# Agent attention and a squared-gate layer on one core: scores and agent values as two 64-column halves, and eight key groups ahead of tile 0

## The chip, the core and the metric

The program runs on one core of one Trainium2 chip. The core has a matrix engine (TensorE; PE in the profile, its weight loads PEld), VectorE (DVE), ScalarE (ACT), GpSimd (POOL), and SyncE (SP), which issues every DMA of this kernel. The metric is the device time of one execution in microseconds (us), lower is better. The kernel before ran three times: 1067.81, 1068.59 and 1078.64 us, median 1068.59.

## What is computed

```python
B, N, C, n_agents = 2, 12480, 128, 49
def sm(a, b):                       # row softmax of scaled scores
    s = (a @ b.transpose(0, 2, 1)) / np.sqrt(C)
    e = np.exp(s - s.max(-1, keepdims=True))
    return e / (e.sum(-1, keepdims=True) + 1e-09)
agent_v = sm(agents, k) @ v         # per batch: 49 x 128
attn = sm(q, agents) @ agent_v      # per batch: 12480 x 128
x = attn.reshape(B * N, C)          # 24960 tokens
h = x @ w_in                        # 128 -> 2048
g = np.where(h >= 1, h, np.where(h <= -1, 0, (h + 1) ** 2 / 4))
out = g @ w_out                     # 2048 -> 128
```

The weights w_in and w_out are 64-bit floats that the kernel decodes itself. All else is float32. A plain float32 matmul is two matmul instructions (each with its own weight load) on the engine; the large products of the second layer are instead split into a high and a low part of a rounded type (fp32r), one instruction each.

## The kernel before

The tokens of both batches are cut into 49 **tiles** of 512 (tile 24 holds the border between the batches, tile 48 has 384). The keys of one batch are 98 blocks of 128, in 14 **groups** of 7 (KG = 7), and the values likewise.

**Startup (batch 0).** For each key group: load (448 KB), scores of the 7 blocks against the agents on PE (L510; the block is the stationary operand, 128 columns; the agents of both batches, 98 columns, stream), copy to `ks` on ACT, running maximum on DVE. Then subtract the maximum (POOL), exponential (ACT), and agent values (L634: 98 columns of `ks` stationary, 129 columns of a value block streaming, summed in PSUM over the 7 blocks of a group and added to `acc` on DVE). From `acc` the agent values `av` are formed, transposed, multiplied with w_in (L699) and split into `w_hi` and `w_lo`. DVE, ACT and POOL decode w_in and w_out beside this.

**A tile.** Its query scores are four blocks (L958: a query block is stationary, 49 agent columns stream); maximum, subtraction, sum and reciprocal on DVE (L973 to L991), exponential on ACT, product on POOL (L996), four transposes on PE (L1009), copies on ACT and DVE to `mt`. Then eight pairs of hidden blocks: first product on PE (L1086; 49 of the 128 rows of the array for each of two row halves, which run side by side), relu and square on ACT (L1094, L1099), gate on DVE (L1102), high part on POOL or DVE, low part on POOL or DVE (L1113), second product on PE (L1126; two row halves of 64). ACT and DVE collect `total`, and SP stores it.

**Rides (batch 1).** The key and value groups of batch 1 are worked off between tiles 3 and 24: in each tile the query scores of the next tile (q) and the transposes of this one (tr) stand next to each other on PE, and each of the two places can carry one **ride**, a key group (L766, 7 matmuls), a value group (L859, 7 matmuls) or a step of what follows them. The order of the rides is the list `order` in `second_batch`; 14 key groups come first, then the maximum, then 14 value groups, then the product with w_in.

**What sets the order.** Every step is an `Op` with its engine, a cost in us, what it depends on and a key. `Order.run` lays them out once, engine by engine, by these numbers (START, NEXT and TIMES hold the keys), and each engine works its list in order. A PE step with another number of array rows than the one before costs `SWITCH` in the plan. On the chip nothing is reordered: an instruction that waits holds up all behind it on its engine.

## Time and profile before

| | value |
|---|---|
| median of three runs | 1068.59 us |
| the profiled execution, its own time | 1067.88 us |
| its span | 1066.0 us |
| PE busy | 1048.2 us (98%) |
| ACT busy | 900.6 us (84%) |
| DVE busy | 860.8 us (81%) |
| POOL busy | 700.6 us (66%) |

The span is the time from the first to the last instruction of the profile; 1.9 us of the profiled execution lie outside it. Busy times are unions over an engine's instructions. Matmuls are pipelined and the ends of their rows are modelled, so a stretch of matmuls is read by the distance from one start to the next. PEclk is the granted clock of TensorE as a share of full speed.

### The profile page before, as it was taken

To read this page: it belongs to the slowest core of one execution; us is meant where nothing else is said; L and a number is where in the kernel's file an instruction comes from. 1 tells how busy PE (TensorE), PEld (TensorE's weight loads), DVE (VectorE), ACT (ScalarE), POOL (GpSimd) and SP (SyncE) were. 2 spreads that over 40 slices of the span, in tenths; PEclk is the share of its full clock that TensorE was granted. 3 is DMA by queue.
4 is the path that set the end of the run, shared out by engine and by line. 5 is a ranking of instruction groups with operands and counts; after the bars stand their busy time and mean duration, and the time that the engine had idled before them with its cause. 6 is when DMAs were issued, how large, how long until landed. Compare 5 with 4: busy or idle time off the path is not lost.

```text
span 1066.0 us, 20344 instructions
## 1 busy us (share of the span) xinstructions
PE 1048.2 (98%) x8117; PEld 797.8 (75%) x8117; DVE 860.8 (81%) x1071; ACT 900.6 (84%) x1003; POOL 700.6 (66%) x442
## 2 busy tenths in 40 slices
PE   7989999999999999999999999999999999999997
PEld 6956777877777777777777877777777777777776
DVE  6677777777887777788888888888888888888886
ACT  2357888778988888799899899999999999999995
POOL 2745666556785676656667767677676776766765
PEclk9979999999999999999999999999999999999999
DMA  9931111200012111000010100101001000000000
GB/s 310 403 141 38 56 55 57 81 30 21 21 52 79 56 56 56 31 30 22 20 41 22 31 30 21 40 21 31 30 21 40 21 30 32 21 28 11 11 21 18
DMA packets 23710, 56.90 MB, mean 53 GB/s; under 512 B 2752, under 2 KB 3136, under 8 KB 23616
## 3 DMA queue, kind: packets, MB, share of 16 engines
q1 hardware_dynamic: 23616, 55.60, 15.4%
q8 instruction: 64, 1.05, 0.4%
q14 instruction: 30, 0.25, 0.1%
HBM read 42.81 MB, written 12.78 MB: 52 GB/s over the span
## 4 chain that ended last, share of the span: by engine, by line
PE 88%; ACT 3%; DVE 2%; POOL 2%; issue 2%; DMA 1%; POOLq 0%; SPq 0%; DVEq 0%; ACTq 0%
PE total L1126 50%; PE ph L1086 23%; PE ph L958 5%; PE ph L859 2%; PE ph L766 2%; PE ph L634 2%; PE ph L1009 2%; ACT g L1094 1%; POOL glo L1113 1%; ACT g L1099 1%; POOL ghi L322 1%; DVE g L1102 1%; PE ph L510 1%; DMA raw<-w_out 1%; DMA kbuf<-kT 0%
## 5 line engine op out<-in xcount | busy, mean ns | idle before, releaser
L1102 DVE SCALAR_TENSOR_TENSOR g<-g,ph 128x1024 f32<-128x1024 f32 (+1 forms) x392 | 470.0, 1210 | 109.3 <-ACT g L1099 87.1
L1094 ACT ACTIVATE g<-ph,half 128x1024 f32<-128x1024 f32 (+1 forms) x392 | 423.7, 1106 | 11.2 <-PE ph L1086 2.8
L322 POOL CAST ghi<-g 128x1024 fp32r<-128x1024 f32 (+1 forms) x196 | 250.5, 1278 | 242.3 <-DVE g L1102 234.3
L1099 ACT ACTIVATE g<-g 128x1024 f32<-128x1024 f32 (+1 forms) x392 | 402.2, 1053 | 6.2
L1113 POOL TENSOR_TENSOR glo<-g,ghi 128x1024 fp32r<-128x1024 f32 (+1 forms) x147 | 352.9, 2401 | 66.9 <-PE ph L958 43.6
L1086 PE MATMUL ph<-mt,w_hi 49*128 49x512 f32 (+2 forms) x1600 | 270.8, 416 | 4.9 <-DVE g L1102 3.8
L1126 PE MATMUL total<-ghi,wo_hi 64*128 64x512 f32 (+1 forms) x1176 | 205.4, 426 | 0.8 <-POOL ghi L322 0.8
L1086 PEld LDWEIGHTS ph<-mt,w_hi 49*128 49x128 f32 x1600 | 151.1, 187 | 64.1 <-issue 22.0
L1126 PE MATMUL total<-g,wo 64*128 64x512 f32 (+1 forms) x784 | 185.4, 591 | 0.1
L1126 PE MATMUL total<-ghi,wo_lo 64*128 64x512 f32 (+1 forms) x1176 | 185.0, 391 | 0.0
L1113 DVE TENSOR_TENSOR glo<-g,ghi 128x1024 fp32r<-128x1024 f32 (+1 forms) x147 | 177.1, 1231 | 1.9 <-POOL ghi L322 1.9
L1126 PE MATMUL total<-glo,wo_hi 64*128 64x512 f32 (+1 forms) x1176 | 174.0, 401 | 0.2 <-POOL glo L1113 0.2
L1086 PE MATMUL ph<-mt,w_lo 49*128 49x512 f32 (+2 forms) x800 | 157.8, 388 | 0.0
L1126 PEld LDWEIGHTS total<-ghi,wo_hi 64*128 64x128 f32 x1176 | 112.8, 185 | 44.1 <-issue 22.6
L1126 PEld LDWEIGHTS total<-ghi,wo_lo 64*128 64x128 f32 x1176 | 112.4, 184 | 24.0
L1126 PEld LDWEIGHTS total<-glo,wo_hi 64*128 64x128 f32 x1176 | 108.4, 186 | 27.3 <-POOL glo L1113 0.6
L1126 PEld LDWEIGHTS total<-g,wo 64*128 64x128 f32 x784 | 75.3, 187 | 55.3 <-issue 46.2
L1086 PEld LDWEIGHTS ph<-mt,w_lo 49*128 49x128 f32 x800 | 77.0, 186 | 15.9
L996 POOL TENSOR_TENSOR pq<-qd,qsm 128x392 f32<-128x392 f32 (+1 forms) x49 | 58.0, 1184 | 25.4 <-DVE qsm L991 25.4
L324 DVE CAST ghi<-g 128x1024 fp32r<-128x1024 f32 (+1 forms) x98 | 71.0, 725 | 1.8
L958 PEld LDWEIGHTS ph<-ag,qt 128*128 128x128 f32 (+1 forms) x392 | 48.0, 193 | 21.2 <-issue 20.7
L958 PE MATMUL ph<-ag,qt 128*128 128x49 f32 (+1 forms) x392 | 54.0, 282 | 4.4 <-DMA qt<-qT 4.4
(102 smaller groups left out, 611.7 us busy)
## 6 DMA issues: line engine op xcount, KB each, us to landing
qt<-qT SPq DMA_DIRECT2D x48, 256.0 KB, 2.7
outT<-ot SPq DMA_DIRECT2D x48, 256.0 KB, 2.0
kbuf<-kT SPq DMA_DIRECT2D x27, 448.0 KB, 4.8
vbuf<-v_in SPq DMA_DIRECT2D x18, 451.5 KB, 4.2
ghi<-v_in SPq DMA_DIRECT2D x5, 451.5 KB, 7.9
glo<-v_in SPq DMA_DIRECT2D x5, 451.5 KB, 9.1
raw<-w_in SPq DMA_DIRECT2D x4, 512.0 KB, 5.8
raw<-w_out SPq DMA_DIRECT2D x4, 512.0 KB, 7.9
```

The costliest lines, as they stand in the source:

```text
L322: pool.tensor_copy(out, in_)
L324: dve.tensor_copy(out, in_)
L634: nc.tensor.matmul(out=one(PS["v", b, g])[0:A2, 0:C + 1], lhsT=ksf[:, g, t * A:t * A + A2], rhs=vb[0][:, t, :], start=t == 0, stop=t == KG ...
L766: nc.tensor.matmul(out=ps[:, t * A:(t + 1) * A], lhsT=kb[:, t * SUB:(t + 1) * SUB], rhs=ag[:, b, :], start=True, stop=True,)
L958: nc.tensor.matmul(out=ps[lo:hi, i * A:(i + 1) * A], lhsT=st["q"][:, i * 128 + lo:i * 128 + hi], rhs=ag[:, b, :], start=True, stop=True,)
L996: (pool if e == "POOL" else dve).tensor_tensor(out=pq[:, :, :, 0:A], in0=d.unsqueeze(2).to_broadcast([128, ns, 2, A]), in1=st["sm"].unsque ...
L1086: nc.tensor.matmul(out=st["h"][:, c, lo:hi], lhsT=W[b][w][r, f:f + 128], rhs=M[j][r, x, lo:hi], start=(i == 0), stop=(i == 2),)
L1094: act.activation(out=st["g"], in_=st["h"][:, :, 0:n], func=ACTF.Relu, bias=half, scale=0.5)
L1099: act.activation(out=st["g"], in_=st["g"], func=ACTF.Square)
L1102: dve.scalar_tensor_tensor(out=st["g"], in0=st["g"], scalar=1.0, in1=st["h"][:, :, 0:n], op0=ALU.min, op1=ALU.max,)
L1113: (pool if e == "POOL" else dve).tensor_tensor(out=st["lo"], in0=st["g"], in1=st["hi"].bitcast(F32), op=ALU.subtract)
L1126: nc.tensor.matmul(out=total[:, i, 0:n], lhsT=w[r, f, :], rhs=x[r, c, :], start=begins, stop=LEFT[j] == 0,)
```

## The change

Three things are changed, and the plan is laid out anew with other keys.

1. Scores (of queries and of keys) and agent values use the array as two halves of 64 columns. A score block of 128 columns becomes two matmuls of 64 columns, which write PSUM rows 0 to 63 and 64 to 127 (`columns`). For the agent values, blocks alternate between the two halves, each half sums its own blocks, and DVE adds both halves to `acc`, in two additions where there was one (`beside`, `join_halves`). The stationary operand is 64 columns instead of 98.
2. Eight of the 14 key groups of batch 1 (`early`) run before and during the first products of tile 0, into the PSUM of `total`, with 98 streaming columns; the first second product waits for the last of them (`early_op`). Six groups remain as rides, and the rides behind them move up by eight places.
3. The loads have other keys: key loads now stand first in SP's queue, ahead of w_in, and the query tiles of the startup come later; eight early key loads stand in the startup where there were four.

```diff
+EARLY = 8
-    ag = const.tile([128, B, A], F32, name="ag")
+    ag = const.tile([128, B + 1, A], F32, name="ag")
+    def columns(ps, lhsT, rhs, lo=0, hi=128):
+        for c in range(lo, hi, 64):
+            nc.tensor.matmul(
+                out=ps[c:c + 64], lhsT=lhsT[:, c - lo:c - lo + 64], rhs=rhs, start=True, stop=True
+            )
+    def beside(ps, g, vt, lo, hi):
+        for t in range(lo, hi):
+            c = 64 * (t % 2)
+            nc.tensor.matmul(
+                out=ps[c:c + 64, 0:C + 1], lhsT=ksf[:, g, t * A:t * A + 64], rhs=vt[:, t, :],
+                start=t < 2, stop=t >= KG - 2,
+            )
+    def join_halves(o, ps, first):
+        if first:
+            dve.tensor_copy(acc, ps[0:A, 0:C + 1])
+        else:
+            dve.tensor_tensor(out=acc, in0=acc, in1=ps[0:A, 0:C + 1], op=ALU.add)
+        dve.tensor_tensor(out=acc, in0=acc, in1=ps[64:64 + A, 0:C + 1], op=ALU.add)
...
             def weigh(ps):
                 st["ps"] = ps
-                for t in range(KG):
-                    nc.tensor.matmul(
-                        out=ps[0:A2, 0:C + 1], lhsT=ksf[:, g, t * A:t * A + A2],
-                        rhs=vb[:, t, :], start=t == 0, stop=t == KG - 1,
-                    )
+                beside(ps, g, vb, 0, KG)
...
+        def early(g):
+            kb = kbuf[(b * NG + g) % BUFS["k"]]
+            ps = total[:, g % 2, :]
...
+            def scores(o, e, lo=0, hi=HALF):
+                for t in range(lo, hi):
+                    columns(
+                        ps[:, t * A:t * A + A2], kb[:, t * SUB:(t + 1) * SUB], agf[:, A:A + A2]
+                    )
...
-        for g in range(NG):
-            keys(g, g)
-        maximum(NG + 2)
-        for g in range(NG):
-            values(g, NG + 5 + g)
-        return form(2 * NG + 6)
+        for g in range(EARLY):
+            early(g)
+        for g in range(EARLY, NG):
+            keys(g, g - EARLY)
+        n = NG - EARLY
+        n += n % 2
+        maximum(n + 2)
+        for g in range(NG):
+            values(g, n + 5 + g)
+        return form(n + NG + 6), late["early"]
...
             for i, b, lo, hi in bl:
-                nc.tensor.matmul(
-                    out=ps[lo:hi, i * A:(i + 1) * A],
-                    lhsT=st["q"][:, i * 128 + lo:i * 128 + hi],
-                    rhs=ag[:, b, :],
-                    start=True,
-                    stop=True,
+                columns(
+                    ps[:, i * A:(i + 1) * A], st["q"][:, i * 128 + lo:i * 128 + hi], ag[:, b, :],
+                    lo, hi,
                 )
...
-                j, p, [w_ops[b][2 * p // 4] for b, _, _ in parts(j)], wo_ops[2 * p // (NH // 2)]
+                j, p, [w_ops[b][2 * p // 4] for b, _, _ in parts(j)],
+                [wo_ops[2 * p // (NH // 2)], *([] if j else [early_op])],
             )
```

The order on PE from the last value groups of the startup to the first products of tile 0 (`vbuf` are value blocks, `qt` queries, `av` the agent values, `win` the decoded w_in, `mt` a tile's weights), before:

```order
L634 MATMUL ph<-vbuf_119,ks 98x129 x7
L958 MATMUL ph<-ag,qt 128x49 x8
L678 MATMUL ph<-ident,av_135 128x49
L699 MATMUL ph<-win,avT_136 128x512 x3
L1009 MATMUL ph<-ident,pq_125 113x128 x4
L699 MATMUL ph<-win,avT_136 128x512
L1086 MATMUL ph<-mt,w_hi 128x512 x4
L1086 MATMUL ph<-mt,w_lo 128x512 x2
```

The same place in the change (L348 is `columns`, L356 is `beside`):

```order
L356 MATMUL ph<-vbuf_119,ks 64x129 x7
L348 MATMUL total<-ag,kbuf_114 64x98 x14
L348 MATMUL ph<-ag,qt 64x49 x16
L348 MATMUL total<-ag,kbuf_115 64x98 x14
L696 MATMUL ph<-ident,av_135 128x49
L348 MATMUL total<-ag,kbuf_112 64x98 x14
L717 MATMUL ph<-win,avT_136 128x512 x4
L348 MATMUL total<-ag,kbuf_113 64x98 x8
L1062 MATMUL ph<-ident,pq_125 113x128 x4
L1139 MATMUL ph<-mt,w_hi 128x512 x4
L1139 MATMUL ph<-mt,w_lo 128x512 x2
L348 MATMUL total<-ag,kbuf_113 64x98 x6
```

Four early groups (those into `total`) now stand between the last values and the first product of tile 0; the other four follow between its later first products.

The order on PE where q and tr of a tile carry two value groups, before:

```order
L958 MATMUL ph<-ag,qt 128x49 x4
L859 MATMUL ph<-vbuf_116,ks 98x129 x7
L859 MATMUL ph<-vbuf_117,ks 98x129 x7
L1009 MATMUL ph<-ident,pq_126 113x128 x4
```

and in the change:

```order
L348 MATMUL ph<-ag,qt 64x49 x8
L356 MATMUL ph<-vbuf_116,ks 64x129 x7
L356 MATMUL ph<-vbuf_117,ks 64x129 x7
L1062 MATMUL ph<-ident,pq_126 113x128 x4
```

Nothing moved within the place: the same steps stand in the same order, with 64 columns each, and the transposes behind them still use the whole array. From tile 25 on, each engine's list is that of before in the same order.

The order on SP around the first loads, before:

```order
L468 DMA ag<-agT 128x98
L953 DMA qt<-qT 128x512
L439 DMA raw<-w_in 128x1024 x2
L487 DMA kbuf_112<-kT 128x512
L487 DMA kbuf_112<-kT 128x384
L487 DMA kbuf_113<-kT 128x896
```

and in the change:

```order
L494 DMA ag<-agT 128x98
L495 DMA ag<-agT 128x49
L516 DMA kbuf_112<-kT 128x512
L516 DMA kbuf_112<-kT 128x384
L516 DMA kbuf_113<-kT 128x896
L516 DMA kbuf_114<-kT 128x896
L516 DMA kbuf_115<-kT 128x896
L464 DMA raw<-w_in 128x1024 x2
```

The first two parts of w_in and the first query tile moved behind four key groups. Up to and with the last value group of batch 0, SP's queue then holds the agents (0.07 MB), 14 key groups (6.42 MB), the four parts of w_in (2.10 MB), one of w_out and one query tile (0.79 MB), and 14 value groups (6.47 MB), 15.85 MB in all.

## Rows read from the trace of the kernel before

**Rows 1.** The page: span, busy time and share by engine, granted clock in 40 slices.
```profile
span 1066.0 us, 20344 instructions
...
PE 1048.2 (98%) x8117; PEld 797.8 (75%) x8117; DVE 860.8 (81%) x1071; ACT 900.6 (84%) x1003; POOL 700.6 (66%) x442
...
PEclk9979999999999999999999999999999999999999
```

**Rows 2.** Windows of one tile: length, busy time by engine, granted clock, DMA, GB/s.
```profile
388.69:410.92 22.23, 22.23 (x178) 17.17 (x178) 16.90 (x22) 18.63 (x22) 15.01 (x10) 1.00 0.22 67
...
900.76:919.88 19.12, 19.12 (x150) 14.07 (x150) 16.32 (x20) 17.77 (x20) 13.43 (x8) 1.00 0.09 28
```

**Rows 3.** Timeline of PE, q and tr without rides: start, length, matmuls.
```profile
568.59 0.63 PE L1126 MATMUL total<-ghi,wo_lo 64*128 64x512 f32 x4
569.06 0.62 PE L1126 MATMUL total<-glo,wo_hi 64*128 64x512 f32 x4
569.61 1.09 PE L958 MATMUL ph<-ag,qt 128*128 128x49 f32 x8
570.54 0.66 PE L1009 MATMUL ph<-ident,pq 128*113 128x128 f32 x4
571.13 0.72 PE L1126 MATMUL total<-glo,wo_hi 64*128 64x512 f32 x4
```

**Rows 4.** Timeline of PE, two value groups as rides.
```profile
403.48 3.31 PE L859 MATMUL ph<-vbuf,ks 128*98 128x129 f32 x28
406.63 0.60 PE L1009 MATMUL ph<-ident,pq 128*113 128x128 f32 x4
```

**Rows 5.** Timelines of three very short windows, tile 24's border block of queries.
```profile
550.65 0.14 PEld L958 LDWEIGHTS ph<-ag,qt 128*64 128x64 f32 x2
...
550.65 0.20 PEld L958 LDWEIGHTS ph<-ag,qt 128*64 128x64 f32 x4
...
550.90 0.19 PEld L958 LDWEIGHTS ph<-ag,qt 128*128 128x128 f32 x1
```

**Rows 6.** Timeline of PE, the narrowest matmuls in row halves (192 columns).
```profile
580.40 0.36 PE L1086 MATMUL ph<-mt,w_hi 49*128 49x192 f32 x4
580.60 0.28 PE L1086 MATMUL ph<-mt,w_lo 49*128 49x192 f32 x2
```

**Rows 7.** Timeline of PE, two key groups as rides and what follows them.
```profile
228.52 1.09 PE L958 MATMUL ph<-ag,qt 128*128 128x49 f32 x8
229.45 3.29 PE L766 MATMUL ph<-ag,kbuf 128*128 128x49 f32 x28
232.57 1.08 PE L1009 MATMUL ph<-ident,pq 128*113 128x128 f32 x4
233.59 2.78 PE L1126 MATMUL total<-glo,wo_hi 64*128 64x512 f32 x12
```

**Rows 8.** Windows of the startup.
```profile
0.00:40.00 40.00, 33.70 (x257) 30.92 (x258) 28.83 (x67) 11.25 (x25) 16.69 (x23) 1.00 0.95 341
0.00:60.00 60.00, 53.68 (x433) 50.58 (x433) 40.96 (x96) 17.23 (x36) 30.21 (x35) 1.00 0.97 360
60.00:90.00 30.00, 25.10 (x119) 14.56 (x121) 23.61 (x33) 22.37 (x27) 14.17 (x11) 0.77 0.11 38
```

**Rows 9.** Timelines of the startup, one engine each.
```profile
6.98 0.43 DVE L380 TENSOR_SCALAR dhi<-raw 128x512 int32<-128x512 int32 x1 [0.27 <-DMA raw<-w_in]
...
35.77 1.72 PE L634 MATMUL ph<-ghi,ks 128*98 128x129 f32 x14
...
35.97 0.46 ACT L320 ACTIVATE ks<-ph 128x343 f32<-128x343 f32 x1 [1.39 <-PE ph L510]
...
58.30 0.28 DVE L650 TENSOR_TENSOR acc<-acc,ph 49x129 f32<-49x129 f32 x1 [1.27 <-PE ph L634]
...
59.20 0.96 DVE L675 TENSOR_SCALAR av<-acc,rs 49x128 f32<-49x128 f32 x1
...
67.48 0.73 PE L1086 MATMUL ph<-mt,w_hi 49*128 49x512 f32 x4
```

More of the change, by code (lines that the diff above doesn't have):

```diff
@@ L467, in agent_attention_moe, with load_agents @@
     warm_op.rel = (("h", warm_op),)
[L468 removed]
+    def load_agents(o, e):
+        nc.sync.dma_start(out=ag[:, 0:B], in_=agT)
+        nc.sync.dma_start(out=ag[:, B:B + 1], in_=agT[:, 0:1])
+    ld_ag = add(("DMA", 1.6), load_agents, (), 2 * PRO)
     def keys_phase(b, k_key, v_key, s_key, m_key, a_key, e_key, p_key=0.0, wait=None):
@@ L632, in av @@
                     area(o, ("v", b, g))
-                for t in range(lo, hi):
-                    nc.tensor.matmul(
-                        out=one(PS["v", b, g])[0:A2, 0:C + 1],
-                        lhsT=ksf[:, g, t * A:t * A + A2],
-                        rhs=vb[0][:, t, :],
-                        start=t == 0,
-                        stop=t == KG - 1,
-                    )
+                beside(one(PS["v", b, g]), g, vb[0], lo, hi)
             def av2(o, e, av=av):
@@ L645, in plus @@
             def plus(o, e, g=g):
-                ps = one(PS.pop(("v", b, g)))
-                if g == 0:
-                    dve.tensor_copy(acc, ps[0:A, 0:C + 1])
-                else:
-                    dve.tensor_tensor(out=acc, in0=acc, in1=ps[0:A, 0:C + 1], op=ALU.add)
+                join_halves(o, one(PS.pop(("v", b, g))), g == 0)
             k = a_key(g)
@@ L660, in keys_phase @@
                 last = add(("DVE", 0.2), rescale[1], [rescale[0], last], k + 0.9)
-            last = add(("DVE", 0.2), plus, [x] + ([last] if g else []), k + 1, (), (back,))
+            last = add(("DVE", 0.4), plus, [x] + ([last] if g else []), k + 1, (), (back,))
         return last, av_ops
@@ L765, in scores @@
                 for t in range(KG):
-                    nc.tensor.matmul(
-                        out=ps[:, t * A:(t + 1) * A], lhsT=kb[:, t * SUB:(t + 1) * SUB],
-                        rhs=ag[:, b, :], start=True, stop=True,
+                    columns(
+                        ps[:, t * A:(t + 1) * A], kb[:, t * SUB:(t + 1) * SUB], ag[:, b, :]
                     )
@@ L795, in keys, with evac, gm @@
             RIDES[order[n]] = Ride(0.2215 * KG, [LK[g], ld_ag], scores, follow, (("k", LK[g]),))
+        def early(g):
+            kb = kbuf[(b * NG + g) % BUFS["k"]]
+            ps = total[:, g % 2, :]
+            key = NEXT["early"] + g
+            LK[g] = load(
+                128 * KG * SUB * 4,
+                lambda o, e: nc.sync.dma_start(out=kb, in_=kT[b, :, g * KG * SUB:][:, 0:KG * SUB]),
+                (), PRO + NEXT["kearly"] + g, ("k",),
+            )
+            def scores(o, e, lo=0, hi=HALF):
+                for t in range(lo, hi):
+                    columns(
+                        ps[:, t * A:t * A + A2], kb[:, t * SUB:(t + 1) * SUB], agf[:, A:A + A2]
+                    )
+            def evac(o, e):
+                copy(e, ksf[:, g, 0:KG * A], ps[:, 0:KG * A])
+            def gm(o, e):
+                dve.tensor_tensor(
+                    out=f, in0=ps[:, 0:KG * A], in1=f if g > 1 else ksf[:, 0, 0:KG * A],
+                    op=ALU.max,
+                )
+            x = add(("PE", 0.24 * HALF), scores, [LK[g], ld_ag], key, ("t",))
+            y = add(
+                ("PE", 0.24 * (KG - HALF)), lambda o, e: scores(o, e, HALF, KG), [x], key, (),
+                (("k", LK[g]),),
+            )
+            y.rows = x.rows = 128
+            KE[g] = add(
+                (("ACT", 0.355), ("DVE", 0.42)), evac, [y, wait[g]], key + 0.1, (),
+                () if g else (("t", x),),
+            )
+            if g:
+                KX[g] = add(
+                    ("DVE", 0.42), gm, [KE[g], *([KX[g - 1]] if g > 1 else [])], key + 0.2, (),
+                    (("t", x),),
+                )
+            late["early"] = KX.get(g, KE[g])
         def maximum(n):
@@ L1046, in finish @@
             tr_op = step(
-                "tr", ("PE", 0.11 * ns), lambda o, e: tr(o, e, ride), [x, first], ("m",),
+                "tr", ("PE", 0.137 * ns), lambda o, e: tr(o, e, ride), [x, first], ("m",),
                 (("qs", qs),),
```

38 lines of the change are left out of this document (16 added, 22 removed).

## The prediction

> **What bounds the kernel now.** I read the page first: PE is busy for 1048.2 of 1066.0 us, and its granted clock is full in all slices but the third [rows 1]. A busy PE proves little, so the second view is the table of windows of one tile. In a tile with two value rides PE is busy for all of 22.23 us, ACT for 18.63 and DVE for 16.90; in a tile without rides PE for all of 19.12, ACT for 17.77 [rows 2]. The third view is the timeline of PE there: matmuls start one behind the other with no idle time [rows 3]. So from about 90 us to the end PE alone sets the time, and each microsecond of PE work that goes is a microsecond of the result, until ACT, which is at 93%, gets in the way. The startup is different: in the first 60 us PE is busy for 53.7, DVE for 41.0, and the DMA engines are used for 97%; from 60 to 90 us PE is idle for 4.9 us, and its clock is 0.77 in the mean [rows 8].
>
> **What column halves cost.** In the full width one instruction of a value ride takes 3.15/28 = 0.1125 us (403.48 to 406.63), and a group 14 of these, 1.57 us [rows 4]. Of the query scores eight instructions take 0.93 us (569.61 to 570.54), 0.113 each and 0.03 once [rows 3]. Key rides take 3.12 us for 28, 1.57 with the 0.03 [rows 7].
>
> The trace of before holds column halves already: the block of queries at the border of the batches is cut there into two halves of 64 columns. Two of their weight loads start together and take 0.14 us, all four 0.20, and the next full load starts 0.25 us after the first [rows 5]. So a load in the one half does not wait for the other, and a pair of instructions follows the pair before it by 0.20 - 0.14 = 0.06 us. A score block then costs two such pairs, 0.12 us, where it costs 0.225 now. This is the number on which the forecast rests, and it is read from two pairs only. Its bounds: 0.055 (the 0.20 and 0.14 are rounded) and 0.10, the densest stretch of pairs of any length that the trace shows (row halves with 192 columns, four matmuls in 0.20 us [rows 6]). I take 0.06, since it is the same form of instruction.
>
> A value block streams 129 columns, and there the stream sets the 0.1125 us. Seven blocks in two halves are four steps (the seventh block stands alone), each of two instructions: 8 x 0.1125 = 0.90 us for a group instead of 1.57.
>
> The change adds a change of the array's form. Between the row halves and the scores there is one today: after 569.06 the next matmul comes 0.55 us on, where 0.47 is usual, so 0.08 [rows 3]. From halves to the transposes there is a new one in each tile: in the border block 0.25 - 2 x 0.06 = 0.13 at most [rows 5]. I take 0.10.
>
> **The sum behind 90 us**, on PE alone:
> - Query scores of tiles 3 to 48, 46 times: 0.93 - (8 x 0.06 + 0.03) - 0.10 = 0.32 us, together 14.7.
> - Six key rides that stay: 1.57 - 14 x 0.06 = 0.73, together 4.4.
> - Eight key rides that go to the startup: 8 x 1.57 = 12.6.
> - Fourteen value rides: 0.67 each, 9.4.
> - One drop of the clock: behind the key rides at 228.5 to 232.6 us the transposes took 1.08 us instead of 0.66 and twelve matmuls 2.78 us where four come in 0.47, so some 1.6, together about 1.5 us [rows 3, 7]. That stretch of narrow matmuls, 4.05 us, is the longest of the kernel and becomes 0.51 + 2 x 0.84; I count the drop as gone.
>
> That is 42.6 us. The second additions to `acc` (DVE, 0.28 us [rows 9]) cost nothing there: DVE is busy for 16.9 of 22.23 us [rows 2], and in the shortened tile for 17.5 of 20.6. Without this cover they would be 14 x 0.28 = 3.9 us. ACT's list loses eight copies of keys there.
>
> **The startup.** The chain runs from the first value group on PE (35.77) to the last addition (58.30), `av` (59.20 to 60.16) and the first product of tile 0 (67.48) [rows 9]. The 14 value groups of 1.57 us become 12.6 us of PE work, so PE no longer sets this. Next is the DMA: the queue holds 15.85 MB up to the last value group; 341 GB/s over 40 us are 13.64 MB, and 40 to 60 us ran at 398 GB/s, so it is loaded at 45.6 us [rows 8], and its matmuls end at about 46.5. Next is DVE: it is busy for 41.0 us up to 60 us [rows 8]; its list up to `av` loses the first query tile's early place and some decoding and gains 13 additions, +0.9 us by the durations of its rows, about 42 us. The decoding starts when w_in lands, at 6.98 us now [rows 9], and some 2 us later behind four key groups. So `av` ends at 9 + 41 = 50 us if DVE never waits, and at 60 if nothing is gained; I take 53, 7 us earlier than now.
>
> The early groups are 8 x 14 pairs; with 98 streaming columns a pair is 0.1125 x 98/129 = 0.085, so 1.2 us a group and 9.6 together. Four stand before the first product, where PE has nothing to do (from 46.5 to about 59 us it has some 7 us of other work). Four stand between first products of tile 0, in the 4.9 us of idle time [rows 8]. They give back some of the gain: two or three copies of 0.46 us [rows 9] on ACT, which there is the chain (it is busy for 22.4 of the 30 us [rows 8], nearly all of it from 68 us on), the maxima on DVE, and loads: the eighth early group lands at about 67 us by the same rates, when its products are due. I count 3 us lost, and 1 us won because PE is kept at work and the clock stays up. Net 5 us, with 0 and 10 as the ends.
>
> **Sum.** 42.6 + 5 = 47.6 us. The profiled execution took 1067.88 us, which gives 1020; it stands 0.7 us below the median of the three runs, and I leave that.
>
> **The rivals.**
> - *Pairs come at 0.10 us*, since four instructions a pair can't be delivered faster for long. For it speaks that nothing denser lasts in the trace [rows 6]; against it, that stretch has full loads in both halves, which fill the time anyway. Then the query scores win nothing (0.93 - 0.83 - 0.10), key rides 6 x 0.17 = 1.0, values 9.4, the moved groups 12.6, the clock's drop stays, the startup 3: 26 us, 1042.
> - *Loads run side by side, but the streams take turns.* The starts in [rows 5] don't show the ends. A score pair is then 2 x 0.0425 = 0.085 us (49 columns by the rate of 129): 0.12 x 46 = 5.5; key rides 6 x 0.38 = 2.3; values nothing; moved 12.6; startup 0: 20 us, 1047.
> - *A half's load waits for the other half's matmul* (slower than before). Load 0.055 and stream 0.0425, twice, make 0.2 us a pair: query scores 0.93 - 1.63 - 0.10 = -0.80 each, -37; the key rides that stay -7; values 14 x 0.17 = 2.35 us a group, -11; the startup about -10; with the 12.6 of the moved groups 53 us more, 1121. It decides from 0.13 us a pair on, where the scores alone eat the moved groups. Against it: the four loads in 0.20 us [rows 5], and full loads that follow at 0.1125 us while matmuls on the same rows run [rows 4]. The Trainium skill, page "TensorE: Matmul & The Clock Gate", section "Part 3: Packing small matmuls", says that weight loads overlap running matmuls only in other row groups, and column halves share all rows; by that rule the sum would be this rival's. The trace does not agree with it.
> - *The clock falls behind each tile's narrow stretch* (also slower): 1.5 us each time [rows 7]; 32 of 46 tiles would eat the gain, all of them give 1089. Against it: the stretches of today are longer, and the tiles of [rows 2] stand at full clock.
> - *ACT takes over.* A tile without rides goes to 18.80 us on PE; ACT has 17.77 [rows 2] and must wait within a tile for scores and transposes. If it can't go below 18.9, some 4 us are lost. It widens the range, to 1024.
>
> **How the numbers follow.** The forecast (pairs near 0.06, both halves streaming) has 0.80; its own range is 1013 (0.055 a pair, 10 us at the startup) to 1031 (nothing at the startup, ACT in the way, the drop of the clock stays). Pairs at 0.10 have 0.08, streams by turns 0.06, the two slower rivals 0.02 each, and 0.02 goes to a loss of like size that I don't see. The range, 1010 to 1038, adds to it some 3 us below and 7 above, for a startup that gains or loses more than its bounds and a change of form at 0.13, and leaves out the rivals. About 1% is what a measurement of this kernel can tell from no change: all cases but the last three are faster by more, so faster 0.94, within 1% 0.02, slower 0.04.
>
> **What would show it.** In the timeline of PE a tile's query scores should take about 0.5 us and be followed by the transposes 0.1 us late; two key rides 1.7 us, two value rides 1.8; tiles without rides should follow at 18.8 us, with value rides at 20.6. `av` should end near 53 us and the first product of tile 0 stand at about 60. A step above 0.08 us a pair, value groups near 1.57, or tiles with a PE that waits for ACT would make it wrong.

## The result, and the profile after

The changed kernel takes 1043.45 us (median of 4 runs, 1042.49 to 1044.36), the kernel before 1069.01 (1067.81 to 1078.64) beside it: ratio 0.9744, 95% interval 0.9709 to 0.9779. The forecast was 1020, at most 1038. The sign was right; about half of the gain came. Each time below is the median of that kernel's executions; a single one, of 1407.63 us at a granted clock of 0.654 (the others have 0.98 to 1.00), is left out.

The page of the changed kernel: span, busy time, granted clock, and the chain that ended last by engine.

```profile
span 1041.0 us, 21943 instructions
...
PE 1011.8 (97%) x8897; PEld 798.4 (77%) x8897; DVE 870.8 (84%) x1102; ACT 896.3 (86%) x1000; POOL 699.2 (67%) x442
...
PEclk9989999999999999999999999999999999999999
...
PE 34%; ACT 31%; DVE 15%; issue 8%; POOL 6%; DMA 4%; POOLq 0%; SPq 0%; DVEq 0%; ACTq 0%
```

PE is still busy for 97% of the span (98% in [rows 1]), but it is only 34% of the chain that ended last, where it was 88% before; ACT is 31% and DVE 15%. PE has shorter work now, and in places it waits for other engines. The timeline of PE after the change, a tile's scores and transposes without rides and with two value groups:

```profile
890.91 0.67 PE L348 MATMUL ph<-ag,qt 128*64 128x49 f32 x16
891.51 0.69 PE L1062 MATMUL ph<-ident,pq 128*113 128x128 f32 x4
...
354.36 0.67 PE L348 MATMUL ph<-ag,qt 128*64 128x49 f32 x16
354.87 1.94 PE L356 MATMUL ph<-vbuf,ks 128*64 128x129 f32 x28
356.74 0.69 PE L1062 MATMUL ph<-ident,pq 128*113 128x128 f32 x4
```

From the first score to the transposes it is 0.60 us where it was 0.93 [rows 3], and two value groups take 1.87 us with the change of form behind them (3.15 in [rows 4]). The bare scores take 0.51 us (354.36 to 354.87). So the halves do run side by side, 0.06 us a pair, and the terms of the sum that came from there are right. Windows of one tile after, with two value groups and without rides (the columns of [rows 2]), and the startup's last stretch:

```profile
292.07:313.62 21.55, 21.27 (x185) 15.29 (x184) 17.48 (x24) 18.28 (x21) 15.02 (x11) 1.00 0.20 69
853.69:872.62 18.93, 18.93 (x160) 16.24 (x156) 16.37 (x20) 17.74 (x20) 13.43 (x8) 1.00 0.09 30
60.00:95.00 35.00, 30.42 (x308) 20.20 (x303) 31.32 (x52) 25.00 (x33) 17.17 (x13) 0.95 0.42 137
```

The tile with two value groups fell from 22.23 to 21.55 us instead of 20.56, the tile without rides from 19.13 to 18.93 instead of 18.80. In the startup DVE is busy for 31.3 of 35 us. I take the transposes of tile 2 as the border between startup and tiles. The timelines of PE show them and those of the last tile, before:

```profile
86.76 0.69 PE L1009 MATMUL ph<-ident,pq 128*113 128x128 f32 x4
...
1029.19 0.58 PE L1009 MATMUL ph<-ident,pq 128*113 128x128 f32 x3
```

and after:

```profile
92.44 0.69 PE L1062 MATMUL ph<-ident,pq 128*113 128x128 f32 x4
...
1004.48 0.58 PE L1062 MATMUL ph<-ident,pq 128*113 128x128 f32 x3
```

So the shortfall has two halves: the startup came 5.7 us later where 5 us earlier was forecast, 10.7 us; from there to the last tile's transposes 30.4 us were won (942.43 to 912.04) instead of 42.6, another 12.2 us.

### The profile page after: what moved, and what is told of

The parts are those of the page before. It is cut to its first block, busy times and chain, and to the rows that moved or that the text cites. A ratio compares the mean times of both kernels' runs of the same rounds, so it can differ in the third digit from the quotient of the medians.

```text
span 1041.0 us, 21943 instructions
## 1 busy us (share of the span) xinstructions
PE 1011.8 (97%) x8897; PEld 798.4 (77%) x8897; DVE 870.8 (84%) x1102; ACT 896.3 (86%) x1000; POOL 699.2 (67%) x442
## 4 chain that ended last, share of the span: by engine, by line
PE 34%; ACT 31%; DVE 15%; issue 8%; POOL 6%; DMA 4%; POOLq 0%; SPq 0%; DVEq 0%; ACTq 0%
PE total L1179 20%; ACT g L1147 16%; ACT g L1152 12%; PE ph L1139 9%; DVE g L1155 6%; POOL glo L1166 3%; DVE glo L1166 3%; PE ph L348 2%; DMA kbuf<-kT 2%; DVE ghi L325 2%; DVE ot L1228 2%; ACT ot L321 2%; POOL ghi L323 2%; DVE qd L1029 1%; DMA vbuf<-v_in 1%
## 5 line engine op out<-in xcount | busy, mean ns | idle before, releaser
L1139 PE MATMUL ph<-mt,w_hi 49*128 49x512 f32 (+2 forms) x1600 | 279.1, 417 | 5.2 <-DVE g L1155 2.3
L1139 PEld LDWEIGHTS ph<-mt,w_hi 49*128 49x128 f32 x1600 | 158.8, 185 | 59.4 <-issue 20.3
L1179 PE MATMUL total<-ghi,wo_lo 64*128 64x512 f32 (+1 forms) x1176 | 190.8, 391 | 0.0
L1139 PE MATMUL ph<-mt,w_lo 49*128 49x512 f32 (+2 forms) x800 | 164.6, 386 | 0.0
L1179 PEld LDWEIGHTS total<-ghi,wo_hi 64*128 64x128 f32 x1176 | 123.9, 185 | 33.0 <-issue 20.6
L1179 PEld LDWEIGHTS total<-ghi,wo_lo 64*128 64x128 f32 x1176 | 123.6, 184 | 13.1
L1179 PEld LDWEIGHTS total<-g,wo 64*128 64x128 f32 x784 | 81.3, 185 | 51.4 <-issue 42.0
L1139 PEld LDWEIGHTS ph<-mt,w_lo 49*128 49x128 f32 x800 | 84.0, 184 | 8.4
L1036 ACT ACTIVATE qd<-qd 128x196 f32<-128x196 f32 (+1 forms) x49 | 17.9, 366 | 41.1 <-DVE qd L1029 41.1
L1228 DVE TENSOR_TENSOR ot<-ot,total 128x512 f32<-128x512 f32 (+1 forms) x49 | 33.5, 684 | 18.9 <-ACT ot L321 18.9
```

Of the source, the lines that this page charges most:

```text
L1139: nc.tensor.matmul(out=st["h"][:, c, lo:hi], lhsT=W[b][w][r, f:f + 128], rhs=M[j][r, x, lo:hi], start=(i == 0), stop=(i == 2),)
L1179: nc.tensor.matmul(out=total[:, i, 0:n], lhsT=w[r, f, :], rhs=x[r, c, :], start=begins, stop=LEFT[j] == 0,)
L1228: dve.tensor_tensor(out=st["o"], in0=st["o"], in1=total[:, 1, 0:n], op=ALU.add)
```

## Experiments: the parts alone

Three kernels do a part of the change in the order and with the loads of the kernel before. The edits here and below are shown in excerpts.

**Scores only** (`columns` for queries and keys; no early groups).

```diff
+def columns(ps, lhsT, rhs, lo=0, hi=128):
+    for c in range(lo, hi, 64):
+        nc.tensor.matmul(
+            out=ps[c:c + 64], lhsT=lhsT[:, c - lo:c - lo + 64], rhs=rhs, start=True, stop=True
+        )
```

> The kernel before with its scores alone (queries and keys) in two 64-column halves; values in full width, no early groups, loads and every engine's list as before. Theory (halves run side by side, a pair every 0.06 us; what the change lost was lost to other engines and in the startup): tiles without rides go from 19.13 to about 18.92 us as in the changed kernel, tiles with two key rides from 22.27 to about 20.3, tiles with two value rides by 0.2 only; some 20 us behind 90 us and nothing in the startup, where keys wait for their loads: 1046 us. Rival (the halves were slow and the gain of the change came from the early groups and the loads): at most 4 us, 1064.

Measured: 1048.07 us, ratio 0.9793 (0.9764 to 0.9822), 2 us above the theory's number: most of the change's gain is here. Tiles without rides take 18.93 us, as the theory has it, but tiles with two key rides 21.08 instead of 20.3; PE stands for 0.3 us in each of them.

**Values only** (`beside` and the second addition).

```diff
-                out=ps[0:A2, 0:C + 1], lhsT=ksf[:, g, t * A:t * A + A2], rhs=vt[:, t, :],
+                out=ps[c:c + 64, 0:C + 1], lhsT=ksf[:, g, t * A:t * A + 64], rhs=vt[:, t, :],
```

> The kernel before with its agent values alone in two halves and added in two additions; scores in full width, the lists of PE, ACT, POOL and SP as before, DVE's with the added additions. Theory (a loop over ACT, DVE and POOL holds a tile with value rides at about 21.6 us): seven tiles go from 22.23 to 21.6, 4 to 5 us, though PE has 1.3 us less to do in each; the startup wins up to 8 us, since PE's 1.57 us a value group set it; 1057 us. Rival (PE alone sets these tiles): 21.0 us a tile, 9 us there.

Measured: 1067.51 us, ratio 0.998 (0.9952 to 1.0009): nothing, though by the prediction's 0.67 us a group PE's value work fell by 9 us in the startup and 9 us in the rides. The window of a value tile:

```profile
317.50:339.42 21.92, 21.86 (x178) 15.92 (x177) 17.49 (x24) 18.40 (x21) 15.26 (x11) 1.00 0.20 67
```

The value tiles went from 22.23 to 21.9 us only, where the theory had 21.6, and the transposes of tile 2 came 2.5 us later, where it had a gain. Neither the theory's 1057 nor the rival's 9 us came: in the tiles a limit other than PE lies close under PE, and in the startup the shorter work on PE brought nothing forward (`av` at 60.47 instead of 59.20).

**Both halves, old order** (no early groups, old loads).

> The kernel before with scores and values in halves, no early groups, loads and lists as before (DVE's with the added additions). Theory (halves win, the early groups and the new order of the loads lost the startup): both gains together, 1037 us, below the changed kernel's 1043, with the first product of tile 0 near 60 us. Rival (the early groups are what won, 8 rides less): above the changed kernel, 1050 or more.

Measured: 1046.31 us, ratio 0.9776 (0.975 to 0.9802): above the changed kernel, as the rival has it, but by 3 us and not by 7, so neither forecast is met. Value tiles are 21.55 us here too. With the decode of w_out where it stands, the early groups and the new loads together are worth the 3 us between 1046.3 and 1043.4: up to the transposes of tile 2 they cost 4.0 us (88.41 and 92.44), behind them they win 7.6 (919.65 and 912.04).

## Experiments: the tile with two value groups

The chain of waits of the changed kernel through one such tile (start, length, what):

```profile
309.26 1.07 ACT g L1152
310.33 0.02 issue
310.35 1.23 DVE g L1155
311.59 0.02 issue
311.61 0.70 DVE ghi L325
...
312.45 2.37 POOL glo L1166
314.82 0.83 POOL ks L899
315.65 0.02 issue
315.67 0.12 ACT ks L906
```

PE is not in it. (`glo` is the low part, `ks` the keys' scores of the ride; L899 is the subtraction of the maximum, L906 the exponential.) ACT's last square goes through DVE's `gate` and `ghi` and POOL's `glo` and two subtractions back to ACT's exponential, which stands in ACT's list ahead of everything of the next tile. The list of waits in this tile, and the same line of the kernel before in its tile of [rows 2]:

```profile
ACT ks L906 <- POOL ks L899: 3.1, 1, 3.1
```

```profile
ACT ks L847 <- POOL ks L840: 3.1, 1, 3.1
```

ACT's 18.28 us of work and 3.1 us of waiting are 21.4 of the 21.55 us. Before, it was 18.63 and 3.1, 21.7 of 22.23: the same wait, hidden under PE by half a microsecond. First try: the subtractions go to DVE.

```diff
             def sub(o, e):
-                (pool if e == "POOL" else dve).tensor_tensor(
+                dve.tensor_tensor(
```

> The changed kernel with one edit: the subtraction of the key maximum for the second batch's value groups (two per value-ride tile, 0.85 us each on POOL) is issued on DVE, at the same place of the program's order. Theory: the seven value-ride tiles last 21.55 us because ACT stands 3.1 us a tile before the exponential that waits for POOL's subtraction, which stands behind POOL's glo (2.37 us), which waits for DVE's ghi, which waits for ACT's square: a loop, not PE. On DVE the subtraction comes about 1.4 us earlier, the loop opens, and the tile falls to PE's own work of it, 20.6 to 20.9 us; 7 tiles by 0.65 to 0.95 us are 4.5 to 6.5 us, so 1037 to 1039. Rival: DVE, which gets 0.9 us more work a tile, is where the tile is held next; the tile stays at 21.3 us or more and the time within 2 us of 1043.

Measured: 1049.2 us, ratio 0.9777 (0.9738 to 0.9816), slower than the change, and the tile 22.69 us; neither the theory's number nor the rival's. The timelines of DVE and POOL of this run:

```profile
295.39 1.42 DVE L899 TENSOR_TENSOR ks<-ks,mb 128x343 f32<-128x343 f32 x1
...
298.65 0.83 DVE L899 TENSOR_TENSOR ks<-ks,mb 128x343 f32<-128x343 f32 x1
```

```profile
294.07 2.37 POOL L1166 TENSOR_TENSOR glo<-g,ghi 128x1024 fp32r<-128x1024 f32 x1 [1.15 <-DVE ghi L325]
```

The subtraction lasts 1.42 us beside POOL's `glo` and ends 0.37 us behind it (296.81 and 296.44); the last section has what it takes without POOL beside it. It comes no earlier than on POOL, and now DVE's list stands behind it. The same edit in the kernel before:

> The kernel before with the same one edit (the second batch's subtractions on DVE). Theory: its value-ride tiles of 22.23 us are PE's own work; ACT's wait of 3 us for the same subtraction was hidden beside it. No difference: 1068 to 1070, value tiles 22.2 us. Rival: these tiles too were held by the loop over POOL, so they fall by 0.3 us or more each (14 groups in 7 tiles: 2 us or more, below 1067).

Measured: 1072.34 us, ratio 1.0002 (0.9967 to 1.0037), and value tiles of 22.23 us, as the theory has it: before, this wait cost nothing.

Second try: the subtractions (collected in `SUBS`) stay on POOL and go one place forward, ahead of the `glo` that they stood behind.

```diff
     ops = od.run()
+    for x in sorted(SUBS, key=ops.index):
+        i = ops.index(x)
+        before = [n for n in range(i) if ops[n].engine == "POOL" and ops[n] not in SUBS][-1]
+        if x.engine == "POOL" and ops[before].tag and ops[before].tag[0] == "lo":
+            ops.insert(before, ops.pop(i))
```

> The changed kernel with the two subtractions of each value-ride tile moved one place forward in POOL's list: ahead of the glo that they stood behind (POOL stands 1.15 us idle there, waiting for DVE's ghi), instead of onto DVE. Nothing else moves. Theory: the tile of 21.55 us is a loop of ACT's square, DVE's gate and ghi, POOL's glo and its two subtractions, and ACT's exponential, which stands in ACT's list ahead of everything of the next tile; with the subtractions ahead of glo the exponential need not wait for glo, ACT loses its wait of 3.1 us, and the tile falls to PE's own work, 20.6 to 20.9 us: 4.5 to 6.7 us in seven tiles, 1037 to 1039. (On DVE the subtraction took 1.42 instead of 0.42 us, until POOL's glo beside it had ended, so that it came no earlier: this is why that edit failed by this theory.) Rival: the tile is held by the row of DVE's small operations between PE's two rides and mt, which grew by two additions; then it stays above 21.3 us and the time within 2 us of 1043.

Measured: 1042.17 us, ratio 0.9718 (0.9687 to 0.9748). The window of such a tile:

```profile
291.22:312.57 21.35, 21.29 (x185) 15.30 (x185) 17.86 (x24) 18.28 (x21) 15.46 (x11) 1.00 0.21 69
```

The wait for POOL is gone, but only 0.2 us of the tile with it: the rival's numbers are met. The list of waits names the next row:

```profile
ACT mt L321 <- DVE acc L367: 2.9, 1, 2.9
```

and the chain of waits shows where it goes (`qd` are query scores less their maximum, `ot` is the output):

```profile
293.03 0.02 issue
293.06 0.30 DVE acc L367
...
293.44 0.10 ACT mt L321
293.54 0.39 issue
293.94 0.36 ACT qd L1037
294.30 0.38 ACT ks L906
294.68 0.49 ACT ot L321
295.17 0.02 issue
295.19 0.70 DVE ot L1229
```

The second ride's result and the transposed weights lie in one PSUM tile, and in the program's order ACT's copy into `mt` stands behind DVE's additions of that ride; it waits for them. They were one, now they are two. Behind the copy stand ACT's copy of the output and DVE's join, and PE's first product of the tile needs these. So two rows of waits lay there, one right under the other. The next two kernels take the second away alone and both together; `PLUS` holds the additions, `copies` the copies into `mt`.

```diff
+    copies = {o.deps[0]: o for o in ops if o.tag and o.tag[0] == "mc"}
+    for x in PLUS:
+        if x.deps[0] in copies and ops.index(x) < ops.index(copies[x.deps[0]]):
+            ops.remove(x)
+            ops.insert(ops.index(copies[x.deps[0]]) + 1, x)
```

> The changed kernel with one edit: in each value-ride tile ACT's copy of the tile's weights into mt is put ahead of DVE's two additions of the second ride in the program's order, so that it waits for PE's transposes only and no longer for these additions (they now wait for it). Theory, as the subtractions moved ahead of glo left it (tile 21.34 us): two rows hold the value-ride tile, first the one over POOL's glo and subtractions, 21.55 us, and right under it the one over DVE's additions, ACT's mt, qd, ks and ot, DVE's join and PE's first product, 21.34 us. With the second alone loosened the first still stands: tiles 21.5 to 21.6 us and 1042 to 1044. Rival: the additions alone hold the tile; then it falls by 0.5 us or more and the time to 1040 or below.

Measured: 1043.53 us, ratio 0.9742 (0.9697 to 0.9787), as the theory has it:

```profile
291.93:313.47 21.54, 20.90 (x186) 16.86 (x185) 17.48 (x24) 18.27 (x21) 15.05 (x11) 1.00 0.22 69
```

> The changed kernel with both edits to its value-ride tiles: subtractions ahead of glo, and the copy into mt ahead of the second ride's additions. Theory: with both rows loosened PE's own work is left, 20.6 to 20.95 us a tile (21.35 less the 0.49 us that PE stood before its first product); 7 tiles by 0.6 to 0.95 are 4.2 to 6.7 us, 1037 to 1039.5. Rival: a third row stands close under the second; tiles above 21.2 us, the time 1041 to 1043.

Measured: 1037.97 us, ratio 0.9692 (0.965 to 0.9733). The window of such a tile:

```profile
289.94:310.57 20.63, 20.63 (x185) 15.43 (x185) 17.86 (x24) 18.56 (x21) 15.50 (x11) 1.00 0.21 71
```

One edit alone gives 0.2 us a tile, the other nothing, both 0.92; PE is busy for all of 20.63 us, where 20.6 was forecast. So the theory is shown: the value groups lost their gain to two rows of waits. The first, the 3.1 us before ACT's exponential, is in the kernel before as well, where PE's longer work covers it; the second, ACT's wait for the additions, is 0.2 us there and 2.9 once the first is gone.

## Experiments: the startup

In the changed kernel PE waits 4.17 us for the first query tile, whose load now stands late:

```profile
50.37 0.79 PE L348 MATMUL ph<-ag,qt 128*64 128x49 f32 x16 [4.17 <-DMA qt<-qT]
```

In what follows g1 and g2 are the first and the second product of a tile, and `LQ` holds the loads of the query tiles. The loads of q0 and q2 are exchanged:

```diff
     ops = od.run()
+    x, y = ops.index(LQ[0]), ops.index(LQ[2])
+    ops[x], ops[y] = ops[y], ops[x]
```

> The changed kernel with two loads of the startup exchanged: the first query tile loads ahead of the values, where the third stood, and the third in its place; every engine's list stays. Theory (the values' last four groups stood behind the first query scores on PE, which waited 4.2 us for their load): that wait goes, av and the first product of tile 0 come 3 to 5 us earlier, 1039 us. Rival (DVE or the early groups set the startup anyway): less than 1 us, 1043.

Measured: 1043.34 us, ratio 0.9751 (0.9718 to 0.9783), as the rival says. The timelines of DVE and PE:

```profile
57.01 0.43 DVE L405 TENSOR_SCALAR dhi<-raw 128x512 int32<-128x512 int32 x1 [4.65 <-DMA raw<-w_out]
...
59.42 1.95 PE L348 MATMUL ph<-ag,qt 128*64 128x49 f32 x32 [4.99 <-DVE mt L1072]
```

PE's wait for the load is gone, and the wait moved to DVE: it stands before a late quarter of w_out, whose decode stands in DVE's list among the last additions to `acc`. In the kernel with both halves in the old order it is alike (2.9 us for that load, `av` at 59.50). So the decode of the last two quarters (`chains[2:]`) is moved behind `avT` and among the four `w_lo` (`points`), in both kernels:

```diff
+    points = [lows[0].deps[0].deps[0].deps[0], *lows]
+    end = max(place[o] for o in points)
+    moved = sorted((o for c in chains[2:] for o in c if place[o] < end and o.choices[0][0] != "DMA"), key=place.get)
+    ops = [o for o in ops if o not in moved]
+    n = -(-len(moved) // len(points))
+    for i, p in enumerate(points):
+        at = ops.index(p) + 1
+        ops[at:at] = moved[i * n:(i + 1) * n]
```

> The kernel with both halves and the old order (no early groups, old loads; 1046.31 us) with the same move: the decode of the last two quarters of w_out behind avT and among the four w_lo. Theory: av at 53 to 55 us instead of 59.50, the first g1 at 63 to 65 instead of 68.98, the time 1040 to 1043. Rival: the last values' loads hold the additions (av at 58 or later), and the time stays within 2 us of 1046.

Measured: 1047.03 us, ratio 0.9762 (0.9716 to 0.9809). `av` comes at 54.10 us and the first g1 at 64.37, as the theory has it; but the first g2 comes at 79.94 (81.01 without the move), and the time is that of the rival. The timeline of ACT shows one reason, a copy of the decoded w_out that stands in its list ahead of three copies to `w_hi`:

```profile
62.48 0.63 ACT L1227 ACTIVATE wo_hi<-wf 128x512 fp32r<-128x512 f32 x1 [3.44 <-POOL wf L440]
63.01 0.58 ACT L320 ACTIVATE w_hi<-ph 128x512 fp32r<-128x512 f32 x1
```

> The changed kernel with the loads of q0 and q2 exchanged and, in the order of DVE, ACT and POOL, the decode of the last two quarters of w_out moved from among the last additions to acc to behind avT and the four w_lo. No instruction is added or taken away. Theory: in the startup the agent values end where DVE, which works its list in order, gets past the wait for a late quarter of w_out (4.65 us at 51.7 us with the loads of q0 and q2 exchanged), not where PE ends; so av comes at 55 to 57 us instead of 62.5, the first g1 at 65 to 67 instead of 71.55, and the time is 1036 to 1041. Rival: the additions wait for PE or for the values' loads as well, or the early groups hold the first g1: g1 stays at 70 us or later and the time within 2 us of 1043.

Measured: 1043.42 us, ratio 0.9722 (0.9683 to 0.9761): `av` at 57.89 (62.53), the first g1 at 69.45, the first g2 at 86.94 (86.27), the numbers in brackets without the move: 4.6 us are won at `av`, 2.1 at g1, and nothing arrives at g2.

In the second form the moved operations have later places (`low` is the last `w_lo`; the last entry is for ACT's copies and POOL's `wo_lo`):

```diff
+    for c, points in (
+        (chains[2], [low] * 7 + [first_tile["square"][1]]),
+        (chains[3], [first_tile["gate"][n] for n in (0, 1, 2) for _ in range(2)]
+         + [first_tile["gate"][2], first_tile["square"][4]]),
+    ):
```

> Both halves in the old order, again with the decode of the last two quarters of w_out behind the agent values, but later: the third behind the last w_lo, the fourth two operations at a time behind the first three gates of tile 0, and the copies to wo_hi and wo in ACT's list behind the second and the fifth square (in the first try they stood ahead of w_hi and held it until 63 us). Theory: DVE's and ACT's lists set the startup; av stays at 54 us, the first g1 comes at 61 to 64 us (68.98 without the move), the transposes of tile 2 3 to 6 us earlier than at 88.41, and the time is 1040 to 1043. Rival: DVE's sum of work up to the first g2 sets it, whatever its order; what is won at av is lost to the gates of tile 0, the transposes of tile 2 come at 86 or later and the time is 1044 to 1046.

Measured: 1044.31 us, ratio 0.9738 (0.9706 to 0.977). `av` 53.61, the first g1 61.48, the first g2 76.87, the transposes of tile 2 85.66 instead of 88.41: 5.9 us won at `av`, 7.5 at g1, 4.1 at g2, 2.7 at tile 2. Between theory and rival: the wait is real, but what is won at `av` drains away on the way to tile 2. DVE, POOL and ACT still have the decode to do there beside tile 0; and the granted clock of TensorE is 0.54 from 65 to 80 us (0.91 in the changed kernel), so that the first products of tile 0 that fall there run at little over half speed. How much each of the two takes isn't shown.

Together with the subtractions ahead of `glo`, in either kernel:

> The last two edits together on the kernel with both halves in the old order: late decode, and the subtractions of its value-ride tiles ahead of glo. If both theories hold: 1046.3 less 3 to 6 less 4.5 to 6.7, 1034 to 1039. If only the loop's: 1039.6 to 1042.

Measured: 1042.48 us, ratio 0.9727 (0.9693 to 0.9762), 0.5 us above the worse of the two ranges: from tile 2 on the loop's edit alone wins little in this kernel too (918.71 us, 919.65 without it).

> The last two edits together on the changed kernel (with the loads of q0 and q2 exchanged): the third quarter's decode behind the last w_lo, the fourth's between the first gates, and the subtractions ahead of glo. If both theories hold: the early groups' maxima and copies share DVE with the decode here, so less is won in the startup, 1 to 4 us, and 4.5 to 6.7 from the loop: 1033 to 1038. If only the loop's: 1037 to 1039.

Measured: 1044.64 us, ratio 0.9748 (0.97 to 0.9796), worse than expected: with the early groups the moved decode makes tile 2 later (95.15 us, against 84.42 in the kernel without them).

With the copies ahead of the additions as well, the kernel without early groups:

> Both halves in the old order (no early groups), late decode in its second form, and both edits to the value-ride tiles. With 20.6 to 20.95 us a value-ride tile: 1042.5 (the same without the copy's edit) less 7 times 0.4 to 0.75, 1037 to 1040, beside 1037 to 1039.5 for the changed kernel with the same two edits: the early groups are then worth no more than the late decode is without them. Rival: 1041 or more.

Measured: 1038.22 us, ratio 0.9694 (0.9654 to 0.9733), not to be told from the 1037.97 above. From the transposes of tile 2 to those of tile 48 the kernel with early groups is 8.1 us shorter (906.39 and 914.52 us), and to tile 2 it is 8.6 us longer (93.19 and 84.60). Beside a late decode the early groups, with the loads that came with them, are worth nothing; the 3 us that they won above stand against the 2 us that the late decode wins without them (1046.31 and 1044.31).

The last two kernels ask which engine pays for them; each starts from the 1037.97 us.

```diff
             def gm(o, e):
+                if g > 1:
+                    return
```

> The changed kernel with both edits to its value-ride tiles (1037.97 us), where DVE leaves out six of the seven running maxima over the early key groups (0.5 us each, 3.0 us, so the maximum of the second batch is taken without these groups). Theory: the startup of the changed kernel from 60 to 95 us is set by DVE's list, in which these maxima, the late decode of w_out and the gates of tile 0 stand one behind the other; 3 us less there bring the first g2 from 86.97 to 83.5 to 85 us, the transposes of tile 2 as much earlier, and the time to 1034 to 1036. Rival: PE's own early matmuls set it; no change (first g2 at 86.5 or later, 1037 to 1039).

Measured: 1036.4 us, ratio 0.9692 (0.9661 to 0.9722).

```diff
             def scores(o, e, lo=0, hi=HALF):
+                if g > 1:
+                    return
```

> The same kernel, all maxima in, where PE leaves out the matmuls of the early key groups 2 to 7 (168 matmuls, some 10 us of PE in the startup; their scores are then not computed). Theory (DVE's list sets the startup): the forms and the first g1 come up to 3 us earlier because nothing of PE stands before them waiting for DVE's maxima, but the first g2 no more than 2 us earlier than 86.97, and the time 1036 to 1038. Rival (PE sets it): the first g2 5 us or more earlier, 1033 or below.

Measured: 1036.87 us, ratio 0.9703 (0.9677 to 0.9729). In time the two can't be told from each other, nor surely from 1037.97. The first g2 comes at 85.56 us without the maxima, where 83.5 to 85 was expected, and at 85.96 without the matmuls (86.97 in the full kernel). In both the first query tile landed late, so that `av` came at 64.0 us instead of 62.34. Counted from there, the first g2 comes after 24.63 us in the full kernel, 21.56 without 3.0 us of DVE's maxima, and 22.01 without 10 us of PE's matmuls; the transposes of tile 2 after 30.85, 28.29 and 30.20. This last number can't be held against PE, for the clock fell in that run. The windows of the full kernel and of the one without the matmuls:

```profile
80.00:90.00 10.00, 8.48 (x94) 5.53 (x92) 8.42 (x12) 8.13 (x10) 4.65 (x3) 1.00 0.45 136
```

```profile
80.00:90.00 10.00, 8.77 (x32) 4.36 (x32) 9.44 (x13) 8.77 (x10) 4.66 (x4) 0.50 0.00 0
```

At 0.50, the lower of its two levels (1.2 GHz), TensorE takes 2.79 us for the first eight second products, where the full kernel takes 1.42. Up to the first g2, less work for DVE is worth 3.1 us and less work for PE 2.6, each in one execution. Which of the two the early groups lengthen stays open.

## Why the prediction was wrong

**Right: the halves.** 0.06 us a pair, 0.51 us for a tile's scores, 0.94 us for a value group with its share of the change of form (0.90 forecast without it). The rivals of slower pairs, of streams by turns and of a load that waits for the other half all fall with the 0.60 us from scores to transposes, and that of a clock that falls behind each tile with the 1.00 in the windows of the tiles. The drop of the clock behind the key rides [rows 7] went, as counted (granted clock 1.00 in every tile from tile 2 on); the timeline of PE, scores, a key group and the transposes behind it:

```profile
165.46 0.99 PE L348 MATMUL ph<-ag,kbuf 128*64 128x49 f32 x28
166.37 0.69 PE L1062 MATMUL ph<-ident,pq 128*113 128x128 f32 x4
```

The transposes take 0.69 us where they took 1.08, and the key group 0.91 with the change of form, 0.84 forecast without it. The rule of the Trainium skill, page "TensorE: Matmul & The Clock Gate", section "Part 3: Packing small matmuls", by which such loads would not overlap, does not hold for these rows.

**Wrong: ACT's slack in a value tile.** This is the step that failed in the tiles. It reads "each microsecond of PE work that goes is a microsecond of the result, until ACT, which is at 93%, gets in the way", and it took ACT's busy time, 18.63 us, for the floor. ACT's floor was its busy time and its wait in a loop, 21.7 us, and the wait stood in the list of waits of the kernel before. The price of the additions, "cost nothing there" since DVE is busy for 16.9 of 22.23 us, failed in the same way: not DVE's sum counted, but the 0.3 us that each addition put in front of ACT's copy (the edit moved both additions of a ride, so the share of the added one isn't measured by itself). Both rows of waits together cost 5.7 us from tile 2 on (912.04 less 906.39 us). The rival "ACT takes over" looked for this in the tiles without rides and put 4 us on it.

**Wrong in size: the tiles without rides.** 0.20 us won instead of 0.33: the scores gave their 0.33 us, but the change of form ahead of the scores, the transposes, and the products right behind them are each some hundredths of a microsecond longer. Over some 29 tiles at 0.13 that is 3.8 us. Of the 2.7 us that are left of the 12.2, 0.6 stand in each of two tiles with key rides (21.08 and 20.26 us, where 20.48 and 19.64 follow from the sum); some 1.5 us I can't place.

**Wrong: the startup.** The step "I take 53" for `av` took DVE's busy time up to there (9 + 41, where the sentence before has 42) and let the waits between be small. `av` came at 61.6 us: DVE works its list in order, and in it stood a query tile whose load had been put off (DVE waits 2.9 us for its scores) and, once that load was exchanged, a quarter of w_out that landed at 57 us. With the decode moved, `av` comes at 53.61 in the kernel without early groups, but at 57.89 with them. And "the first product of tile 0 at about 60" and the rest do not follow from `av` alone: from 60 to 95 us DVE has decode, gates and, with the early groups, maxima and copies to do, 31.3 of 35 us. The "3 us lost" to the early groups were 4.0 against the old order as it was and 8.6 against the old order with late decode. Behind tile 2 the eight groups won 7.6 to 8.1 us; the 12.6 of the sum are for groups at full width, of which the halves alone would have won a part. The clock stayed up as the prediction has it, 0.95 from 60 to 95 us against 0.77 from 60 to 90 us in [rows 8]; whether that is worth the 1 us put on it, no run shows.

The chance of 0.94 for faster was well founded; the range was not. Its upper end, 1038, let the startup lose its gain but gave the tiles behind nearly all of theirs.

## What to carry to other kernels

When the busiest engine gets shorter work, the new floor of a stretch is not the busy time of the next engine but its busy time and the waits that it has in a loop with others; read these waits in the list of waits before the change, although they cost nothing there. Two such rows can lie one right under the other, so an edit that takes away one and moves the time little is no proof against it: take both away before the theory is given up. In a startup, look at what stands in an in-order list ahead of the operation that is awaited, and when its load lands, before work is added there. And before two stretches are compared, compare their granted clocks: taking matmuls out of PE's list lowered the clock for the matmuls that were left.

## What the runs showed of the hardware

A subtraction of 128x343 on DVE, both of whose inputs are in SBUF, took 1.42 us when POOL worked on other tensors beside it, and ended 0.37 us after POOL's operation (296.81 and 296.44); the second one of the same tile took 0.83 us and ended 0.37 us after POOL's `ghi` (299.48 and 299.11). In the kernel before with the same edit, POOL was idle when the subtraction began (its `ghi` began at 354.64), and it took 0.50 us; the 0.42 that the expectation above names as its length is measured nowhere. The timeline of DVE there:

```profile
354.43 0.50 DVE L840 TENSOR_TENSOR ks<-ks,mb 128x343 f32<-128x343 f32 x1
```

Moving work from POOL to DVE did not free it from POOL. The Trainium skill, page "SBUF — State Buffer", section "SBUF: two separate sides", says that a DVE operation with two SBUF inputs and a GpSimd operation that reads SBUF hold a shared pair of ports against each other for the whole instruction, and that the other blocks; the two ends in this trace agree with it, and the edit had not reckoned with it.

The clock behind the key rides at full width fell in some executions and not in others. Five tiles with two key rides stood at full clock in the profiled execution of the kernel before; in that of the kernel before with the subtractions on DVE, an edit that touches value tiles alone, the same five had 0.93. One such tile in each:

```profile
143.48:165.76 22.28, 22.28 (x178) 18.11 (x178) 17.17 (x22) 18.66 (x21) 13.45 (x8) 1.00 0.22 66
```

```profile
151.71:175.46 23.75, 23.75 (x177) 18.61 (x178) 17.21 (x22) 18.54 (x21) 13.40 (x8) 0.93 0.20 61
```

That is 1.5 us a tile. With scores in halves no such tile fell below full clock in any profiled execution, and the executions of each such kernel, three to five of them, lie within 5 us of each other; each of the three kernels with key rides at full width spreads over 11 to 16 us, in ten executions or more. So the 1.5 us that the prediction counted for the clock is what one execution showed, and others give up more.

The best kernel of the study is the changed one with the two edits to its value tiles, 1037.97 us, 0.9692 of the kernel before; without the early groups and with the late decode it is 1038.22.
